# A state-space mixer with an MLP gate: the second group's rows in two transfers, and another order of the instructions

## The chip, the core and the metric

The kernel runs on one core of a Trainium2 chip. The core has five instruction streams that matter here: TensorE (PE: matmuls; its weight loads are shown apart, as PEld), VectorE (DVE), ScalarE (ACT), GpSimd (POOL) and SyncE (SP, which here only issues DMA transfers). Each stream runs its instructions in the order in which they were written, and waits on semaphores for the others. The metric is the time of one execution on the device in microseconds (us); a kernel's time is the median of its runs.

## What is computed

For 2048 tokens of width D = 448 the kernel normalises x, runs the result through a diagonal complex recurrence (A) and, separately, through a second normalisation and an MLP with F = 1792 (B), and gates one with the other. Cut to what matters:

```python
def _A_ref(x, ...):                       # the recurrence over the tokens
    dt = jnp.exp(log_dt)
    Lam_bar = jnp.exp(dt * Lam)
    B_bar = ((Lam_bar - 1.0) / Lam)[:, None] * Bmat
    Bu = einsum("bld,pd->blp", x, B_bar)
    h_t = Lam_bar * h_{t-1} + Bu_t
    return 2.0 * einsum("bld,dp->bld", h, Cmat).real + x * Dskip

def _B_ref(x, w1, b1, w2, b2):
    h = gelu(layernorm(x) @ w1 + b1)
    return h @ w2 + b2

xn = layernorm(x)
out = x + _A_ref(xn, ...) * silu(_B_ref(xn, ...))
```

## The kernel before

**Tiling.** The 2048 tokens are 8 blocks of 256; two blocks are a group, and there are four groups. In a block the even and the odd tokens ("par" 0 and 1) form the two halves of 128 rows, one token pair in each partition. Each group goes through the same stages:

- *Rows in.* `ldx` (a DMA that SP issues; every plain transfer is recorded by the helper at L84) brings x to `x_all`. Block 0 comes as two transfers, block 1 as one, and from then on two blocks come in one transfer of 448 KB.
- *Normalisation.* Statistics (L401, aggregated at L407; L431 and L432 for the first group), the scale (L478 to L488; Ln and Exp on ACT at L434, L435, L438 and L439 for the first group), and its application to `xn_sb` and `xn2_sb` (L499 on VectorE or L500 on ACT; L453 for the first group). The normalised rows are transposed to `xnT` and `xn2T`, for the first group's MLP by TensorE (L460, copied out at L419), otherwise by DMA (helper L83).
- *MLP.* `mm1_run` (L809) multiplies by w1 in phases: 64-row matmuls, six of the first kind and eight of the second, into a pair of PSUM banks. The gelu (L813, two activations on ACT) empties the pair, and only then can the next phase start on it. There are three such pairs. `mm2` (L836) has 14 matmuls for each 128 rows, into bank 5 or 6; then VectorE adds b2 (L839) and the silu follows (on ACT, or as tanh on ACT and a product on VectorE).
- *Recurrence.* `bu` (L737, bank 4) gives Bu, copied out by L419. `ssm` (L752 to L783) is a long chain on VectorE: products, the scans (L761, L763), copies to `s_b` (L419 on ACT or VectorE), and products again into `h_sb` (L779, L781, L783).
- *Output.* `ym` multiplies h by C (L879 for par 0, with L882; L879 with L885 for par 1) into bank 7 (in the last group 7, 4 and 0). VectorE takes it from there (L891, L893, L896), an add (L899) brings x in, and SP sends the rows out. The products xn times Dskip (`xd`, L855 and L856) and, for the last one, L864 serve the odd rows.

Once, between the first and the second group's work, the kernel makes the tables of the recurrence, the matrices `BT`, `CQ` and `CZ`, and the matrix M0 (L720 for the first three quarters; `m0_halves`, L705, for the last one, whose operand is CQ and whose bank 7 is emptied by VectorE and ACT).

**What sets the order.** Nothing is emitted where it is written. Each piece of work becomes a task of a `Plan`: an engine, one or more instructions, and the names of what it reads and writes. `link` derives the dependencies from these names. `emit` (L127 to L159) then goes through the list `ORDER` (L162 to L184), 634 task numbers, and puts each task's instructions on its engine with the semaphore waits that its dependencies need. A task recorded with `either` has a second engine to run on; `SECOND` (L185 to L188) lists the 60 tasks that take it. So these two lists alone decide what each engine does, and in which order:

```python
for t in order:
    eng, seen = self.engs[t.eng], self.seen[t.eng]
    ...
    for sem, val in reversed(waits):
        eng.wait_ge(self.sems[sem], val)
    ...
    for k, fn in enumerate(t.ins):
        last = fn(eng)
```

**The start.** TensorE runs warm-up matmuls (L422, on `ones`; 26, 12, 5 and 5 of them) around the first small jobs: the transposes of the parameters Lambda_re, Lambda_im and log_dt (L529, L530), the transposes of the first normalised rows (L460) and b1's columns (L602, L603). ACT issues the three parameter transfers, loads the table for Ln and Exp (L316), and later that for gelu (L443).

**The loads on SP.** x of blocks 0 and 1, then w1 in eight transfers, then `ldx(2, 2, S1 + 7)` (L377, blocks 2 and 3), then w2 in four, then B and C.

Of the kernel before, what the change touches and what calls it, by code (L numbers as in the profile page):

```python
# [155 lines left out]
def dram_ap(t, offset, ap):  # L156
    return bass.AP(tensor=t.tensor, offset=offset, ap=ap)
# [2 lines left out]


ORDER = [int(k) for k in """  # L162
# [17 lines left out]
""".split()]  # L180
SECOND = [int(k) for k in """
46 54 55 62 64 67 70 75 77 84 108 113 131 134 159 161 163 164 166 178 185 186 188 190 191 221 223 225 227 229 231 239 249 250 259 267 269 332 363 365
366 385 401 402 437 448 469 481 483 488 492 500 502 503 505 511 529 530 610 613
""".split()]  # L184


# [14 lines left out]
def bass_recurrent_scan__ssm_conv_s5__mixer_channel_mlp__prompt_kernel(  # L201
# [18 lines left out]
    with ExitStack() as es:  # L220
# [85 lines left out]
        with nc.Block():  # L306
# [26 lines left out]
            def ld(eng, o, i, writes, nbytes, prio, reads=(), dur=0.45):  # L333
                kb.dma(eng, o, i, reads=reads, writes=writes, prio=prio, nbytes=nbytes, dur=dur)
# [4 lines left out]
            def ldx(b0, n, prio, reads=(), eng="sp"):  # L339
                ld(eng, x_all[:, b0:b0 + n, :, :], dram_ap(A_x, b0 * 256 * D, [[2 * D, 128], [256 * D, n], [D, 2], [1, D]]),  # L340
                   [f"x{b}" for b in range(b0, b0 + n)], n * 256 * D * 2, prio, reads, dur=0.25 + 0.2 * n)
# [16 lines left out]
            S1 = 10 * PINNED  # L358
# [12 lines left out]
            for c, (a, n) in enumerate(CH):  # L371
# [2 lines left out]
            ld(("pool", "sp")[0], dbc[:], dram_ap(A_Dskip, 0, [[0, 128], [1, D]]), ["dbc"], 114688, -20, reads=[] if 0 else ["sgn3", "w1r_3"])  # L374
            kb.either(("act", lambda e: e.activation(dbc[:], dbc[:], ACT.Copy, scale=0.5), 0.6, 0.2),
                      ("dve", lambda e: e.tensor_scalar(dbc[:], dbc[:], 0.5, None, op0=ALU.mult), 0.2, 0.12), ["dbc"], ["dbc"], -20)
            ldx(2, 2, S1 + 7)  # L377
            CK = []

            def ldc():  # L380
# [592 lines left out]
            for step in STEPS.split():  # L973
                k, g, a = step[0], int(step[1]), step[2:]
# [54 lines left out]
```

## Time and profile before

| | |
|---|---|
| median of 3 runs | 153.82 us (153.58 to 154.24) |
| the profiled execution | 153.63 us |
| its span | 151.9 us, and 1.73 us around it |
| TensorE granted clock | 1.00 |
| the span's chain on TensorE, by line | L809 29.1%, L836 28.2%, L737 14.3%, L879 12.3%, L882 4.0% |
| bytes moved by DMA | 14.73 MB, 97 GB/s in the mean |

Busy time of an engine is the time in which it runs instructions; issuing DMA transfers is not counted. The chain of waits is followed back from the last instruction: at each step to what released it, or to the instruction ahead of it on its engine. Where the chain stays on one engine, that engine's own work sets the time, and other engines matter only where they make it wait. A row of a timeline has the start, the duration, the engine, the line, the operation, output and inputs with their shapes, the number of instructions, and in brackets the idle time before it with what ended it.

### The profile page before, as it was taken

How to read it: one execution, taken by the hardware profiler on the slowest of the kernel's cores; microseconds unless marked ns; L12 is line 12 of the kernel's file. 1: busy time of each engine (PE TensorE's matmuls, PEld its weight loads, DVE VectorE, ACT ScalarE, POOL GpSimd, SP SyncE). 2: the span in 40 equal slices, each digit the busy share in tenths (PEclk: the TensorE clock that was granted, in tenths of full speed). 3: DMA queues.
4: the chain of work that ended last, by engine and by line, in shares of the span. 5: the costliest groups of instructions: out<-in, count | busy, mean ns of one | idle time of the engine just before them, and what ended most of it. 6: DMA issues, size and time to landing. Idle time of an engine off the chain costs nothing.

```text
span 151.9 us, 2990 instructions
## 1 busy us (share of the span) xinstructions
PE 147.6 (97%) x1136; PEld 87.5 (58%) x1136; DVE 128.2 (84%) x270; ACT 98.4 (65%) x182; POOL 40.8 (27%) x100
## 2 busy tenths in 40 slices
PE   7999999999999999999999999999999999999992
PEld 7886755444566577545444556754444666555561
DVE  3978969899998969999999996379968727999984
ACT  3787998888789559997798610462579833067400
POOL 5377870053021910010366006200071040000200
PEclk9999999999999999999999999999999999999999
DMA  4999999889996100700003032610340001100022
GB/s 117 270 309 389 262 231 182 175 150 154 214 213 165 23 0 0 138 0 4 0 0 63 4 60 53 146 60 4 60 109 14 4 0 60 60 0 0 4 102 79
DMA packets 31236, 14.73 MB, mean 97 GB/s; under 512 B 24752, under 2 KB 30774, under 8 KB 31222
## 3 DMA queue, kind: packets, MB, share of 16 engines
q1 hardware_dynamic: 30912, 14.26, 41.9%
q0 software_dynamic: 160, 0.23, 0.6%
q8 instruction: 9, 0.15, 0.4%
q10 hardware_dynamic: 150, 0.05, 0.1%
q14 instruction: 5, 0.04, 0.1%
HBM read 6.89 MB, written 1.84 MB: 57 GB/s over the span
## 4 chain that ended last, share of the span: by engine, by line
PE 96%; DVE 2%; issue 0%; DVEq 0%
PE psum L809 29%; PE psum L836 28%; PE psum L737 14%; PE psum L879 12%; PE psum L882 4%; PE psum L422 3%; PE psum L720 3%; PE psum L885 1%; DVE t L893 1%; PE psum L460 1%; DVE tmp L899 1%; PE psum L705 1%; PE psum L602 0%; DVE ones L309 0%; PE psum L529 0%
## 5 line engine op out<-in xcount | busy, mean ns | idle before, releaser
L809 PE MATMUL psum<-xn2T,w_sb 64*128 64x512 bf16 (+1 forms) x462 | 44.6, 345 | 0.2
L836 PE MATMUL psum<-w_sb,gT 128*128 128x448 bf16 x224 | 44.4, 353 | 0.0
L813 ACT ACTIVATE gT<-psum,b1f 128x512 bf16<-128x512 f32 (+1 forms) x66 | 36.0, 625 | 10.6 <-PE psum L809 10.4
L809 PEld LDWEIGHTS psum<-xn2T,w_sb 64*128 64x128 bf16 x462 | 24.0, 109 | 19.7 <-ACT gT L813 2.3
L836 PEld LDWEIGHTS psum<-w_sb,gT 128*128 128x128 bf16 x224 | 21.6, 98 | 20.3 <-issue 0.6
L419 ACT ACTIVATE u_sb<-psum 128x512 bf16<-128x512 f32 (+2 forms) x22 | 10.5, 478 | 23.0 <-PE psum L737 22.7
L737 PE MATMUL psum<-xnT,BT 128*128 128x256 bf16 x196 | 24.0, 273 | 0.0
L737 PEld LDWEIGHTS psum<-xnT,BT 128*128 128x128 bf16 x196 | 18.9, 98 | 5.4 <-issue 1.1
L761 DVE TENSOR_TENSOR_SCAN s_w<-dk,vs 128x774 f32<-128x774 f32 x8 | 14.0, 1760 | 0.1
L899 POOL TENSOR_TENSOR tmp<-t,x_all 128x448 bf16<-128x448 bf16 x5 | 5.2, 1031 | 33.1 <-DVE t L896 30.7
L500 ACT ACTIVATE xn_sb<-x_all,lnw 128x448 bf16<-128x448 bf16 (+2 forms) x21 | 13.0, 661 | 1.2 <-DVE xn_sb L499 1.1
L419 ACT ACTIVATE vs<-s_w 64x256 bf16<-64x256 f32 (+2 forms) x16 | 10.9, 682 | 2.6 <-DVE s_w L761 1.5
L879 PE MATMUL psum<-CZ,h_sb 128*128 128x448 bf16 x56 | 11.9, 353 | 0.0
L839 DVE TENSOR_TENSOR o<-psum,b2bc 128x448 f32<-128x448 f32 x16 | 9.7, 614 | 1.7 <-PE psum L836 1.5
L879 PE MATMUL psum<-CQ,h_sb 128*128 128x448 bf16 (+2 forms) x54 | 10.5, 332 | 0.0
L879 PEld LDWEIGHTS psum<-CZ,h_sb 128*128 128x128 bf16 x56 | 5.4, 98 | 4.7 <-DVE lnmv L407 0.4
L401 DVE BATCH_NORM_STATS2 lnst<-x_all 128x6 f32<-128x448 bf16 x12 | 7.0, 614 | 0.6 <-DMA x_all<-in_A_x_dram 0.6
L879 PEld LDWEIGHTS psum<-CQ,h_sb 128*128 128x128 bf16 x54 | 5.1, 98 | 4.0 <-DVE t L893 0.4
L882 PE MATMUL psum<-M,xnT 128*128 128x448 bf16 x32 | 7.4, 352 | 0.0
L891 DVE TENSOR_TENSOR Cr<-psum,xd 128x448 f32<-128x448 f32 x7 | 4.3, 620 | 3.5 <-PE psum L885 3.4
L480 POOL TENSOR_TENSOR lnw<-lnw,mhalf 128x8 f32<-128x8 f32 x3 | 7.0, 2332 | 0.3
L499 DVE TENSOR_SCALAR xn_sb<-x_all,lnw 128x448 bf16<-128x448 bf16 (+2 forms) x19 | 6.9, 395 | 0.0
(160 smaller groups left out, 189.8 us busy)
## 6 DMA issues: line engine op xcount, KB each, us to landing
out_dram<-tmp SPq DMA_DIRECT2D x7, 224.0 KB, 2.0
x_all<-in_A_x_dram SPq DMA_DIRECT2D x3, 448.0 KB, 4.3
w_sb<-in_B_w_dram SPq DMA_DIRECT2D x3, 448.0 KB, 8.5
w_sb<-in_B_w_dram SPq DMA_DIRECT2D x3, 384.0 KB, 4.9
vs<-in_A_C_re_dram SPq DMA_DIRECT2D x1, 392.0 KB, 11.5
Bn<-in_A_B_im_dram SPq DMA_DIRECT2D x1, 336.0 KB, 10.4
Bn<-in_A_B_re_dram SPq DMA_DIRECT2D x1, 336.0 KB, 10.8
vs<-in_A_C_im_dram SPq DMA_DIRECT2D x1, 336.0 KB, 11.3
```

What stands on the lines that cost most here:

```text
L401: dve([lambda e, b=b, par=par, q=q: e.bn_stats(lnst[:, q, :], x_all[:, 2 * g + b, par, :])], [f"x{2 * g + b}"] , [f"st{q}"], 0.62, prio)
L419: kb.either(("act", [lambda e, o=o, i=i: e.activation(o, i, ACT.Copy) for o, i in pairs]), ("dve", [lambda e, o=o, i=i: e.tensor_copy(o, i ...
L480: power = fns + [lambda e: e.tensor_tensor(w(2), w(0), mhalf[:].to_broadcast([128, 2, nq]), ALU.pow), lambda e: e.tensor_tensor(w(3), mean ...
L500: ("act", [lambda e, o=o, i=i: e.activation(o, i, ACT.Identity, bias=nb, scale=rs) for o, i in parts], 0.75, 0.2)]
L737: fns = [lambda e, r=r, m=m, d=d: e.matmul(psum[:, 4, r * NK:(r + 1) * NK], BT[:, m, d, :], xnT[:, gx, d, :], start=(d == 0), stop=(d == 6 ...
L761: dve(lambda e, so=so, vi=vi: e.tensor_tensor_scan(so, dk[:].rearrange("p i c -> p (i c)"), vi, 0.0, ALU.mult, ALU.add), ["v", "vl", "dk", ...
L809: return lambda e: e.matmul(view(bk[k]), w1_sb[rows, d, fcol(2 * j + k)], rhs[rows, d, :, :], start=not second and n == 0, stop=second and ...
L813: act([lambda e, k=k: e.activation(gT[:, gb, 2 * j + k, :].rearrange("p (r c) -> p r c", r=2)[:, :, cols], view(bk[k]), ACT.Gelu_apprx_tan ...
L836: fns = [lambda e, fi=fi: e.matmul(psum[:, bk, 0:D], gT[:, gb, fi, q * 128:(q + 1) * 128], w2_sb[:, fi, :], start=(fi == 0), stop=(fi == N ...
L839: dve(lambda e: e.tensor_tensor(o2[:, fb, :], psum[:, bk, 0:D], b2bc[:], ALU.add), [f"ps{bk}", "b2bc"], [f"oo{fb}"], 0.62, prio - 76)
L879: fns = [lambda e, k=k: e.matmul(psum[:, bk, c0:c1], h_sb[:, hb, k, k0:k0 + 128], cm[:, k, c0:c1], start=(k == 0), stop=False) for k in ra ...
L882: fns += [lambda e, d=d: e.matmul(psum[:, bk, c0:c1], xnT[:, gx, d, xs], M0[:, d, c0:c1], start=False, stop=(d == 3)) for d in range(4)]
```

## The change

The one load of blocks 2 and 3 becomes two loads of one block each, so that block 2's work can start when its own half is there. One task more is recorded (635), so the numbers of the tasks behind it grow by one, and the lines behind L377 too (L809 becomes L810). The lists `ORDER` and `SECOND` are new throughout; `SECOND` has 71 entries now.

```diff
 ORDER = [int(k) for k in """
-1 14 20 0 48 10 17 19 21 15 2 95 27 18 96 92 28 93 22 16 25 49 5 97 13 109 94 91 110 98 105 104 26 106 100 23 99 50 51 56 6 52 66 107 3 111 101 112 57
...
+13 0 49 10 16 92 20 96 6 26 97 3 14 19 17 25 93 15 1 21 94 5 27 101 18 23 2 50 95 98 106 110 51 107 111 99 52 102 113 105 53 100 108 112 109 28 54 55
...
 SECOND = [int(k) for k in """
-46 54 55 62 64 67 70 75 77 84 108 113 131 134 159 161 163 164 166 178 185 186 188 190 191 221 223 225 227 229 231 239 249 250 259 267 269 332 363 365
...
+46 53 55 65 68 69 73 76 78 79 82 84 85 86 87 88 90 91 112 132 135 158 160 163 165 179 186 189 191 192 222 224 226 228 230 232 236 238 240 242 248 260
...
-            ldx(2, 2, S1 + 7)
+            for a in (2, 3):
+                ldx(a, 1, S1 + 7)
```

What the new lists do, found by setting the two orders side by side:

- **TensorE** has the same 1136 instructions. At the start the 26 and 12 warm-up matmuls come in one go, then the parameters' transposes, both transposes of block 0, b1's columns, and the last ten warm-up matmuls. The first six L836 matmuls stand ahead of the last six phases (36 matmuls) of the first group's L809. L705 stands before one L836 (14 matmuls) and seven L737 that it followed. The last L836 of the third group stands before the last group's L809, and the L737 of that group's odd-sized tile comes earlier; the outputs of the last two groups are in a slightly different order.
- **ACT** loads its first table before it issues the transfer of log_dt. It has 176 instructions instead of 186.
- **VectorE** has 285 instructions instead of 270. It takes 18 tasks from ACT (five of the scalings at L666, five L500, copies of u and `s_b` and some others) and 21 from POOL (two adds L899, two products L855 and L856, and column-sized operations), and gives 12 tasks to ACT and 16 to POOL (four L856, one L899, the add at L864, and small ones).
- **POOL** has 91 instead of 96, **SP** 60 instead of 59.

More of the change, by code (lines that the diff above doesn't have):

```diff
@@ L162 @@
 ORDER = [int(k) for k in """
[17 rows of a table removed]
[17 rows of a table added]
 """.split()]
 SECOND = [int(k) for k in """
-46 54 55 62 64 67 70 75 77 84 108 113 131 134 159 161 163 164 166 178 185 186 188 190 191 221 223 225 227 229 231 239 249 250 259 267 269 332 363 365
-366 385 401 402 437 448 469 481 483 488 492 500 502 503 505 511 529 530 610 613
+46 53 55 65 68 69 73 76 78 79 82 84 85 86 87 88 90 91 112 132 135 158 160 163 165 179 186 189 191 192 222 224 226 228 230 232 236 238 240 242 248 260
+261 262 268 271 352 354 381 405 446 448 449 452 470 471 481 484 485 489 501 506 507 509 514 527 528 532 533 574 611
 """.split()]
```

32 rows, old and new, of the table ORDER are left out of this document.

## The prediction

> **What bounds the kernel now.** I read the busy times first, then the chain of waits, then stretches of the span.
>
> ```profile
> span 151.9 us, 2990 instructions
> PE 147.6 (97%) x1136; PEld 87.5 (58%) x1136; DVE 128.2 (84%) x270; ACT 98.4 (65%) x182; POOL 40.8 (27%) x100
> ...
> PE 96%; DVE 2%; issue 0%; DVEq 0%
> ```
>
> TensorE is busy for 97% of the span and is the chain for 96% of it; VectorE, at 84%, is the only engine near it. So time can be won only where TensorE waits, and lost wherever an order makes it wait more. The windows by stage (columns: window, length, then busy time of PE, PEld, DVE, ACT, POOL, granted clock, DMA share, GB/s) say where it waits:
>
> ```profile
> 0.00:7.17 7.17, 6.00 (x68) 5.62 (x69) 4.28 (x14) 3.60 (x11) 3.33 (x17) 1.00 0.68 187
> 7.17:19.30 12.13, 12.00 (x176) 8.91 (x176) 10.31 (x41) 10.81 (x24) 8.96 (x26) 1.00 1.06 317
> 19.30:67.50 48.20, 48.20 (x338) 27.77 (x336) 43.64 (x98) 40.06 (x72) 11.84 (x33) 1.00 0.72 128
> ...
> 147.50:151.90 4.40, 1.35 (x15) 1.01 (x12) 2.21 (x6) 0.00 (x0) 0.00 (x0) 1.00 0.31 104
> ```
>
> Before 7.17 us TensorE runs warm-up matmuls while the inputs are normalised; after 147.5 VectorE finishes the last outputs. Between them PE has no gap, at a granted clock of 1.00. Busy is not full cadence, though. The undisturbed pace is readable from the chain: 56 L836 matmuls in 10.70 us are 0.191 each; 14 L737 in 1.53 are 0.109 each. Against such paces, matmul groups after 7.17 lose only about 3.2 us in all: roughly 0.1 at each change between 64-row (L809) and 128-row matmuls, and the rest in a few short waits, most of them at the end of the first group's L809:
>
> ```profile
> 7.17 2.48 PE psum L809 x42
> 9.65 0.55 PE psum L460 x8
> 10.20 7.49 PE psum L809 x102
> 17.69 0.05 issue
> 17.74 0.97 PE psum L809 x14
> 18.71 0.05 issue
> 18.76 0.63 PE psum L809 x8
> 19.39 10.70 PE psum L836 x56
> ```
>
> The two "issue" steps are where the first group's gelu (L813 on ACT) has not freed a PSUM pair: in the weight-load rows the idle gaps before 17.73 and 18.76 are 0.32 and 0.33. By the 0.054 us per matmul of an undisturbed eight-matmul phase (0.43), three phases there (17.17, 18.20, 18.76) lose 0.25, 0.23 and 0.13: 0.61 us. This is what an order can win at once.
>
> **The change, part by part.** PE keeps its 1136 instructions and every shape, so its 147.6 us of work is a floor that stays.
>
> *The split load.* Blocks 2 and 3 come in two transfers of 224 KB instead of one of 448 KB.
>
> ```profile
> 6.78 0.59 SPq L84 DMA_DIRECT2D x_all<-in_A_x_dram  x1
> 12.15 2.21 DVE L401 BATCH_NORM_STATS2 lnst<-x_all 128x6 f32<-128x448 bf16 x4 [0.44 <-DMA x_all<-in_A_x_dram]
> ```
>
> The old transfer is issued at 6.78 and lands at 12.13, where VectorE has waited 0.44 for it. At the 317 GB/s of that stretch half of it is 0.7 us, so block 2 should land near 11.5 and the 0.44 goes. What it feeds is not on the path: these statistics lead to the normalised rows whose transposes PE needs at 30.0 and which landed at 27.24, 2.8 us early. One more issue costs SP 0.59, and every SP transfer behind it (w2, B, C) is issued that much later; but SP runs ahead of the data here (w2's four pieces are issued by 9.30 and land 14.16 to 18.51, needed from 19.3), and the bytes are the same. So 0; without that cover, 0.6 at most, or 0.44 gained at best.
>
> *The start.* ACT now loads its table (1.28) before it issues log_dt; this DMA moves from 1.37 to about 3.0. PE runs 26+12 warm-up matmuls in one go, then the parameter transposes, both x transposes without five matmuls between them, and ten warm-up ones. ACT makes the first half's scale (two activations, 0.53) before the second's, and VectorE puts one block-1 statistic (0.62) ahead of the two normalisations:
>
> ```profile
> 4.44 0.40 DVE L453 TENSOR_SCALAR xn_sb<-x_all,lnmv,lnw 128x448 bf16<-128x448 bf16 x1
> 4.75 0.62 DVE L431 BATCH_NORM_STATS2 lnst<-x_all 128x6 f32<-128x448 bf16 x1
> 5.29 0.38 DVE L453 TENSOR_SCALAR xn_sb<-x_all,lnmv,lnw 128x448 bf16<-128x448 bf16 x1
> ...
> 6.60 0.42 DVE L419 COPY xn2T<-psum 128x512 bf16<-128x512 bf16 x1 [0.17 <-PE psum L460]
> ```
>
> Statistics end at 4.52; first scale 5.08, second 5.57, second normalisation to 5.95 instead of 5.67. The transposes follow at once, to 6.55. VectorE has a statistic and an aggregate in between, so its copy ends near 7.25 instead of 7.02, and L809 starts near 7.40: **+0.23**. The gelu table load ends 0.4 later (9.0); the pair that this gelu frees is next wanted at 10.8, against about 10.7 ready: 0.
>
> *The first L836 in pieces.* Six of the first 14 L836 matmuls (6 x 0.19 = 1.13 us) move ahead of the last six L809 phases, 36 matmuls. That is work PE does while ACT catches up, so the 0.61 goes: ACT still has L500 rows (2.06 for three) among these gelus. It costs two more shape changes at 0.1: **-0.61 + 0.20**. Their w2 piece landed at 15.34; PE comes there near 16.9, so it is there even after one more SP issue.
>
> *Work moved between engines.* By the rows of each kind, VectorE takes 18 tasks from ACT (16.2 us there) and 21 from POOL (9.9), and gives 12 (6.6 on VectorE) to ACT and 16 (4.1) to POOL. What it takes runs faster there (an L499 0.40 against 0.66 for L500; an L899 0.42 against 1.03), so VectorE grows by about 3.5 us to 131.7, ACT falls to about 91. Neither reaches 147, so the totals cost nothing; slack at single points counts. I followed each of VectorE's values up to the PE step that needs it, with the old durations in the new queue. Most have 0.5 us or more left. Tight ones: L705 (M0's last quarter) stands ahead of one L836 and seven L737 now, 3.4 us earlier, and its operand is ready with 0.05 left (0.7 before); L783's second half for the second group's first output has 0.3 (0.7 before); that of the last group 0.06 (0.26 before). I charge **+0.08** for these. The last outputs keep their order on VectorE:
>
> ```profile
> 147.65 0.51 DVE t L893
> ...
> 149.47 0.42 DVE tmp L899
> ```
>
> so the tail stays. A mishap could be one late by a whole VectorE instruction: 0.4 to 0.7 at each.
>
> One pattern speaks against the change: where POOL's and VectorE's two-input operations run together, both stretch.
>
> ```profile
> 111.45 1.44 DVE L896 TENSOR_TENSOR t<-Cr,g_sb 128x448 bf16<-128x448 f32 x1 [1.15 <-POOL tmp L899]
> 113.35 1.20 DVE L763 TENSOR_TENSOR_SCAN s_w<-cw,cur,vs 128x256 f32<-128x256 f32 x1
> ```
>
> The same L896 takes 0.62 at 109.69, the same scan 0.74 elsewhere: +0.82 and +0.46. Now four L856 products go to POOL, one beside the chain before L783. *By the Trainium skill ("SBUF — State Buffer", "Who interferes with whom") a VectorE instruction with two SBUF inputs and GpSimd exclude each other for a whole instruction; the trace agrees as far as these rows go, and by that rule each such meeting costs VectorE up to POOL's 1.03.* POOL's total falls by about 2 us, so there are not more meetings in sum, and I charge nothing; the rival below does.
>
> **Sum.** +0.23 - 0.61 + 0.20 + 0.08 = -0.10 us. The profiled execution took 153.63, its span 151.9 with 1.73 around it; it stands 0.19 below the median of 153.82. So span 151.8, and **153.7** as the median.
>
> **The rivals.** Chances in brackets, 0.42 for the forecast (its own range 153.2 to 154.4).
>
> *B, faster (0.22).* The start is no later, since PE's free run of transposes and VectorE's earlier copies absorb the 0.23, and other first-stage waits go with the 0.61: 0.13 at 10.14 and 0.14 at 34.57. -0.10 - 0.23 - 0.27, and one of the two shape changes free (-0.10), is -0.7: **153.1**, to 152.8 if an add of the tail that POOL takes over (L864, about 0.3 on VectorE) is time won. For it: PE's waits sit just there. Against it: the copy rests on a queue I could follow instruction by instruction.
>
> *C, slower (0.26).* VectorE, with 3.5 us more, comes late at L705, at L783 of the second and of the last group, because locks like those above (0.46 to 0.82) exceed slacks of 0.05, 0.3 and 0.06. All three by 0.64 in the mean: 0.59 + 0.34 + 0.58 = 1.5; the first and the last alone give 1.17, in place of the 0.08 charged: 153.7 + 1.1 = **154.8**; all three and a POOL add beside L893 in the tail (0.4) give 153.7 - 0.08 + 1.5 + 0.4 = 155.5. It decides once these waits exceed 0.9 together. Against it: most late values are caught up, as PE takes other work first.
>
> *D, log_dt late (0.10).* Issued at 3.0 after the table load, and with the 2.0 us minimum from issue to landing in this trace, it lands at 5.0 or later, while PE, after its 38 warm-up matmuls, stands before the parameter transposes from about 5.3; both x transposes (wanted at 5.7) are behind them. A landing at the x transfers' median 2.4 after an issue at 3.2 gives 5.6 plus: 0.1 to 0.8 late, **154.2** at 0.5.
>
> *That the split does nothing* gives the forecast's number, since it was priced at 0.
>
> **How the numbers follow.** A change of under 0.5% (0.77 us) can hardly be told from none here. Faster: B and 0.02 of the forecast, 0.24. Slower: C, half of D and 0.04 of the forecast, 0.35. Same: 0.41. The range reaches from B's end, 152.8, to C's end, 155.5.
>
> **What would show it.** L809's first row at 7.3 to 7.5; no issue step in the chain between 10 and 20 us and L836 appearing near 17; the L401 rows from 11.6 without the DMA wait; DVE near 132, ACT near 91; L705 near 60.4 with no gap in PE. PE's weight loads waiting for DVE at L705 or L879 would mean C; PE idle before L530 means D. I am wrong if PE's busy share drops below 96.5%, or if the time moves by more than 0.77 us from another stage than the first 20 us.

## The result, and the profile after

| | before | after |
|---|---|---|
| median | 153.82 us (153.25 to 154.47, 7 runs) | 155.63 us (154.44 to 156.49, 7 runs) |
| profiled execution | 153.63 us, span 151.9 | 154.78 us, span 152.6 |
| spans of all runs, median | 152.0 (151.5 to 152.9, 29 runs) | 153.4 (152.3 to 154.3, 7 runs) |
| time around the span, median | 1.74 us (29 runs) | 2.18 us (7 runs) |

The change made the kernel slower: ratio 1.0104, 95% interval 1.0065 to 1.0144. The loss of 1.81 us in the medians is 1.4 us of span and 0.4 us around it. The profiled execution of the changed kernel is one of its shorter ones, with 0.7 us of span lost: what the profile shows is about half of the span lost in the median. The changed kernel has seven runs from one session; the 29 of the kernel before were made beside the first experiments.

The lines that answer to those shown of before come first, from the page of the changed kernel:

```profile
span 152.6 us, 3000 instructions
PE 147.5 (97%) x1136; PEld 87.3 (57%) x1136; DVE 132.2 (87%) x285; ACT 91.7 (60%) x172; POOL 40.0 (26%) x95
...
PE 66%; DVE 24%; DMA 4%; issue 2%; ACT 1%; SPq 0%; DVEq 0%; ACTq 0%
```

PE has the same work, but the chain of waits that was 96% PE is now 66% PE, 24% VectorE and 4% DMA: something other than PE set the end for a while. The windows by stage (columns as before) say where:

```profile
7.37:20.34 12.97, 12.97 (x185) 9.60 (x184) 11.92 (x43) 11.50 (x26) 8.05 (x24) 1.00 1.07 319
20.34:48.00 27.66, 27.66 (x204) 15.24 (x204) 23.39 (x59) 23.82 (x39) 8.88 (x27) 1.00 0.98 173
48.00:68.00 20.00, 19.39 (x129) 11.85 (x127) 19.35 (x40) 14.14 (x30) 5.70 (x8) 1.00 0.26 50
68.00:108.78 40.78, 40.78 (x277) 22.20 (x277) 36.59 (x68) 20.03 (x36) 8.79 (x14) 1.00 0.24 42
```

PE is idle for 0.61 us between 48 and 68, and nowhere else between its first L810 and its last matmul:

```profile
48.88 0.36 PE L721 MATMUL psum<-CQ,Bn 128*128 128x448 bf16 x1 [0.61 <-DVE CQ L670]
```

The chain of waits up to there, read from its DMA step on:

```profile
38.95 0.44 SPq L83
39.39 0.04 issue
39.44 4.08 DMA x_all<-in_A_x_dram
...
43.54 1.68 DVE lnst L402 x3
...
45.65 0.58 DVE CQ L670
...
47.57 0.60 DVE CQ L670
48.17 0.09 DVE lnmv L408
48.26 0.58 DVE CQ L670
48.84 0.05 issue
48.88 1.50 PE psum L721 x7
```

The transfer of blocks 4 and 5 (not the one that was split) leaves SP at 39.44, behind the same four transposes of BT as before; before it left at 37.92. Of these 1.5 us, 0.62 are a small piece of B (64 rows) that now precedes the four, and 0.89 are the four themselves (6.40 against 5.51 us); why they took longer is not shown. The transfer lands at 43.52. On VectorE three statistics of these blocks stand ahead of the last three CQ products, and its timeline shows that it stood there:

```profile
41.15 0.68 DVE L670 SCALAR_TENSOR_TENSOR CQ<-Cr,cw,tmp 128x448 bf16<-128x448 bf16 x1
43.54 1.68 DVE L402 BATCH_NORM_STATS2 lnst<-x_all 128x6 f32<-128x448 bf16 x3 [1.72 <-DMA x_all<-in_A_x_dram]
```

The order of before had a statistic ahead of the last three CQ products too, but there the transfer landed 0.20 after VectorE came for it:

```profile
42.26 0.63 DVE L401 BATCH_NORM_STATS2 lnst<-x_all 128x6 f32<-128x448 bf16 x1 [0.20 <-DMA x_all<-in_A_x_dram]
```

The statistics serve the third group, whose first L810 starts at 68; but the products CQ2, CQ4 and CQ6 stand behind them in the same queue, and the first L721 (M0) needs all seven CQ. PE's milestones in the two profiled executions (L809 and its successors, starts in us):

| | first L809 | end of first group's L809 | second group's first L809 | first M0 | third group's first L809 | end of the last matmul |
|---|---|---|---|---|---|---|
| before | 7.17 | 19.39 | 30.02 | 48.40 | 67.51 | 148.85 |
| after | 7.37 | 20.34 | 29.84 | 48.88 | 68.00 | 149.34 |

At 30 us the change is 0.18 ahead; at the first M0 it is 0.48 behind, and it stays 0.49 behind to the last matmul. The other 0.2 us come behind the last matmul. The last output transfer is issued 1.08 us after it in both (149.93 and 150.42), but SP then waits longer for the outputs to land, first before, then after:

```profile
SPq L153 <- DMA out_dram<-tmp: 1.2, 1, 1.2
SPq L153 <- DMA out_dram<-tmp: 1.5, 1, 1.5
```

It is so in every trace: 1.2 or 1.3 us in the five of the order of before and its variants, 1.4 to 1.7 in the ten of the new order. The output ahead of the last three leaves later now (148.03, before 146.81), so more of the bytes are under way at the end; that this is the cause was not tested.

### The profile page after: what moved, and what is told of

Its sections match the earlier page's. It is cut to its first block, busy times and chain, and to the rows that moved or that the text cites. A ratio compares the mean times of both kernels' runs of the same rounds, so it can differ in the third digit from the quotient of the medians.

```text
span 152.6 us, 3000 instructions
## 1 busy us (share of the span) xinstructions
PE 147.5 (97%) x1136; PEld 87.3 (57%) x1136; DVE 132.2 (87%) x285; ACT 91.7 (60%) x172; POOL 40.0 (26%) x95
## 4 chain that ended last, share of the span: by engine, by line
PE 66%; DVE 24%; DMA 4%; issue 2%; ACT 1%; SPq 0%; DVEq 0%; ACTq 0%
PE psum L810 21%; PE psum L837 19%; PE psum L738 10%; PE psum L880 7%; DMA x_all<-in_A_x_dram 4%; PE psum L721 3%; PE psum L883 2%; DVE tmp L668 2%; DVE s_w L762 2%; DVE CQ L670 2%; DVE o L840 2%; DVE tmp L900 2%; DVE lnst L402 1%; DVE Bn L670 1%; DVE t L897 1%
## 5 line engine op out<-in xcount | busy, mean ns | idle before, releaser
L810 PE MATMUL psum<-xn2T,w_sb 64*128 64x512 bf16 (+1 forms) x462 | 44.2, 345 | 0.0
L810 PEld LDWEIGHTS psum<-xn2T,w_sb 64*128 64x128 bf16 x462 | 24.1, 109 | 19.2 <-issue 2.1
L501 ACT ACTIVATE xn_sb<-x_all,lnw 128x448 bf16<-128x448 bf16 (+2 forms) x20 | 12.5, 659 | 0.7 <-DVE xn_sb L500 0.4
L842 ACT ACTIVATE g_sb<-o 128x448 bf16<-128x448 f32 x8 | 4.6, 570 | 9.2 <-DVE o L840 9.1
L420 ACT ACTIVATE vs<-s_w 64x256 bf16<-64x256 f32 (+2 forms) x9 | 6.9, 771 | 3.8 <-DVE s_w L762 3.6
L845 DVE SCALAR_TENSOR_TENSOR g_sb<-th,o 128x448 bf16<-128x448 f32 x8 | 4.9, 614 | 2.0 <-ACT th L844 2.0
L500 DVE TENSOR_SCALAR xn_sb<-x_all,lnw 128x448 bf16<-128x448 bf16 (+2 forms) x20 | 6.6, 365 | 0.0
```

Of the source, the lines that this page charges most:

```text
L420: kb.either(("act", [lambda e, o=o, i=i: e.activation(o, i, ACT.Copy) for o, i in pairs]), ("dve", [lambda e, o=o, i=i: e.tensor_copy(o, i ...
L501: ("act", [lambda e, o=o, i=i: e.activation(o, i, ACT.Identity, bias=nb, scale=rs) for o, i in parts], 0.75, 0.2)]
L810: return lambda e: e.matmul(view(bk[k]), w1_sb[rows, d, fcol(2 * j + k)], rhs[rows, d, :, :], start=not second and n == 0, stop=second and ...
```

## The experiments

All are orders of the same tasks. The runs whose names begin with b_ start from the order of before, those with a_ from the changed one. The pattern of the diffs: rows of one engine's queue, with "-" where a task stood and "+" where it went. "CI" is the 95% interval of the ratio to the kernel before. A pair such as (0,1) is a pair of PSUM banks, CQ5 or BT1 a piece of that matrix; lines behind L377 are one higher where the load is split.

| run | ratio (CI) | median us | span, median | around, median |
|---|---|---|---|---|
| b_split | 0.9988 (0.9969 to 1.0007) | 153.50 | 151.8 | 1.73 |
| a_onedma | 1.0071 (1.0048 to 1.0094) | 154.91 | 152.8 | 2.14 |
| a_stats_late | 1.0005 (0.9989 to 1.0020) | 154.03 | 152.1 | 1.97 |
| a_x4_early | 1.0045 (1.0026 to 1.0063) | 154.63 | 152.4 | 2.17 |
| b_early836 | 1.0042 (1.0026 to 1.0059) | 154.45 | 152.7 | 1.76 |
| a_no836 | 1.0045 (1.0019 to 1.0071) | 154.23 | 152.4 | 1.89 |
| a_start | 1.0005 (0.9983 to 1.0026) | 153.93 | 152.1 | 1.86 |
| b_x4_late | 1.0251 (1.0197 to 1.0304) | 158.19 | 156.4 | 1.79 |
| a_best | 1.0030 (1.0012 to 1.0048) | 154.23 | 152.3 | 1.92 |
| b_best | 0.9971 (0.9955 to 0.9987) | 153.27 | 151.6 | 1.74 |
| a_dbc_late | 1.0045 (1.0022 to 1.0069) | 154.76 | 152.6 | 2.14 |
| a_two_late | 1.0012 (0.9988 to 1.0036) | 154.04 | 152.1 | 1.91 |
| a_all | 1.0024 (1.0003 to 1.0044) | 154.27 | 152.4 | 1.88 |

**Split or order?** b_split is the order of before with the two loads; a_onedma is the new order with the one load.

```diff
 b_split, SP
-x of blocks 2 and 3, 448 KB
+x of block 2, 224 KB
+x of block 3, 224 KB
```

> The order of before with the split load alone: blocks 2 and 3 in two transfers, the second right behind the first on SP, everything else as before. Theory (the loss sits in the order, not in the split): block 2 lands near 11.5 instead of 12.13, VectorE's 0.44 wait for it goes, PE unchanged; ratio to before 0.997 to 1.003. Rival (the split itself costs, as one more transfer ahead of w2, B and C on SP, or as one more transfer to close at the end): 1.005 to 1.010, with PE waiting for w2 or a later stage, or with more than 1.73 us of time around the span.

> The new order with the old single transfer for blocks 2 and 3. Theory (the loss sits in the order): as slow as the change, 1.007 to 1.013, with PE's wait for CQ ahead of the first L721 (0.6 us in the changed kernel) still there. Rival (the split costs): back to 1.000 or below. The time around the span, 2.18 us in the changed kernel against 1.73 before, tells which of the two it belongs to.

The split alone is not distinguishable from no change. Its one profile does show the rival's sign, PE waiting for w2, whose last piece landed at 19.65 (18.51 before):

```profile
PE psum L837 <- DMA w_sb<-in_B_w_dram: 0.7, 1, 0.7
```

But in b_best (below), with the same two loads, that piece landed at 17.57 and PE did not wait, and the median of b_split's spans is no longer than that of before; so this wait is not there in every execution, and the split is not shown to cause it. The order alone costs 0.5 to 0.9%, with PE's wait for CQ (0.7 us in its profile) in it; PE also waited 0.6 there for the first normalised rows. So most of the loss belongs to the order. Whether the split adds something in the new order is open: the intervals of a_onedma and of the change overlap, and their medians are 0.7 us apart. The time around the span (2.14) goes with the order too.

**The wait behind the statistics.** Two ways to take it away, from two sides of it.

```diff
 a_stats_late, VectorE
 L670 CQ5
-L402 and L408, blocks 4 and 5 (eight tasks, between the CQ)
 L670 CQ2 ... CQ4 ... CQ6
+L402 and L408, blocks 4 and 5
```

> The changed kernel with the four statistics and four aggregates of block 4 and 5 (L402, L408) moved behind the last CQ (L670) on VectorE; nothing else moves. Theory (VectorE stood 1.7 us before the transfer of blocks 4 and 5 with CQ queued behind it, and PE then waited 0.6 for CQ): PE's wait goes, every later PE instruction is 0.7 earlier, span near 151.9, ratio to before 1.003 to 1.006. Rival (CQ is late anyway, by VectorE's added work): VectorE's wait only moves, PE still waits 0.4 or more, ratio unchanged at 1.010.

```diff
 a_x4_early, SP
 L83 BT0, BT3
+x of blocks 4 and 5
 L83 BT1, BT4
-x of blocks 4 and 5
 L83 BT2, BT5
```

> The changed kernel with the transfer of blocks 4 and 5 two transposes earlier on SP (issued near 36.8 instead of 39.4), VectorE's queue as it is. Theory: it lands near 40.9, before VectorE asks for it at 41.8; VectorE's 1.7 us wait and PE's 0.6 go, ratio 1.003 to 1.006. Rival (two transposes of BT are now late and PE waits for them instead): a gap before L738 at 42.4 of 0.3 or more, ratio 1.008 or more.

With the statistics late, the span is 152.1 in the median and 1.3 of the 1.4 us is back. That is more than the theory gave (1.003 to 1.006) and twice the 0.6 to 0.7 us that the wait cost in the profile, so a part of it has another source, which is not shown. The spans also vary less (151.6 to 152.4 over twelve runs, against 152.3 to 154.3); but a_no836 and a_start, which have the late statistics too, reach 154.0 and 153.2, so the narrow spread is not owed to them alone. In its profile CQ6 ends at 46.63 and the first M0 follows its neighbour at 48.25 without a gap:

```profile
45.36 1.27 DVE L670 SCALAR_TENSOR_TENSOR CQ<-Cr,cw,tmp 128x448 bf16<-128x448 bf16 x2
46.55 1.67 DVE L402 BATCH_NORM_STATS2 lnst<-x_all 128x6 f32<-128x448 bf16 x3
```

The earlier transfer takes the wait for CQ away as well, and the ratio lies in the theory's range; but the rival's wait came with it: BT is now late, and PE waits 0.4 us for it (from the table of PE's waits of that run):

```profile
PE psum L738 <- DMA BT<-Bn: 0.4, 1, 0.4
```

So moving the transfer pays on one side and costs on the other, and moving the statistics costs nothing that a run shows. The reverse, the suspected cost alone in the kernel before:

```diff
 b_x4_late, SP
 L83 BT, four
-x of blocks 4 and 5
 L83 BT, three
+x of blocks 4 and 5
```

> The order of before with the transfer of blocks 4 and 5 behind three more transposes on SP (issued near 42.4 instead of 37.9, landing near 46.4); VectorE's queue is untouched. This is the suspected cost alone and larger. Theory: VectorE, which asks for it at 42.1, waits 4.1 us more with CQ3's successors queued behind; the last CQ ends near 50.8 instead of 47.28 (a wait of 0.54 before it goes), PE stands 2.3 us before the first L720, ratio 1.012 to 1.018. Rival (VectorE catches up, as PE is the bound): PE's wait under 1 us, ratio under 1.007.

```profile
46.34 0.63 DVE L401 BATCH_NORM_STATS2 lnst<-x_all 128x6 f32<-128x448 bf16 x1 [4.06 <-DMA x_all<-in_A_x_dram]
```

VectorE waited 4.06 and PE 2.0 (2.3 had been expected), and this execution had a span of 154.3. Its other three runs had spans of 156.4 to 156.5, which no trace shows; the ratio of 1.025 is larger than either theory gave.

**A second wait of the same kind.** The change also put the scaling of Dskip (L376) early on VectorE, where it waits for its own transfer (0.52 us in the changed kernel's profile, 1.0 in one experiment and 1.9 to 2.0 in two, as that transfer landed between 19.8 and 22.1).

```diff
 a_dbc_late, VectorE (a_two_late: this and a_stats_late)
 L637 three
-L376 dbc
 L640, L655, L500, L840, L562, L565, L574
+L376 dbc
```

> The changed kernel with one task moved: VectorE's scaling of Dskip (L376), which the change put where VectorE reaches it at 19.9 us and waits for its transfer (landings of 19.8 to 22.1 in the traces so far), goes seven instructions later, behind the first add of b2. The statistics stay where the change has them. Theory (this second wait delays VectorE, and with it CQ, by an amount that varies from run to run): the wait at 20 us goes, VectorE reaches the statistics sooner but still stands before them until the transfer of blocks 4 and 5 lands; CQ still late, ratio 1.004 to 1.009, between the change (1.0104) and the run with late statistics (1.0005). Rival (it costs nothing, as the wait for blocks 4 and 5 absorbs it): ratio 1.010 as before.

> Both moves: late statistics and late Dskip. Theory (both waits of VectorE on transfers cost): ratio 0.997 to 1.000, span no longer than 152.0, no wait of PE for VectorE. Rival (with the statistics late, VectorE has catching up enough): 1.0005 as in the run with late statistics.

a_dbc_late lies between the change and a_stats_late, though its interval touches the change's; PE still waited 0.8 for CQ. With the statistics late, moving L376 too brings nothing (1.0012 against 1.0005). So moving the statistics is enough to bring the lost span back, and L376 can at most feed the same delay.

The profile of a_dbc_late is the one trace of a longer execution of an order so near to the change (span 153.7, 1.1 more than the changed kernel's). There the inputs land later: PE waits 0.3 for the first normalised rows and 0.3 for a piece of w1, its first L810 starts at 7.68, the second group's at 30.59 (29.84 in the changed kernel) and the first M0, behind a wait of 0.83 for CQ, at 49.85 (48.88). So of the 1.1 us about 0.75 arise in the first 30 us, 0.6 of them as these two waits, and 0.2 in a longer wait for CQ.

**The early L836.** The forecast put 0.61 us on PE's waits at the end of the first group's L809, and expected the six early L836 to fill them.

```diff
 b_early836, PE (a_no836 is the reverse, in a_stats_late)
 L809 phases
+L836 x6
 L809 x6 pair (0,1), L809 x8 pair (0,1), L809 x6 pair (4,7), L809 x8 pair (4,7)
-L836 x6
 L836 x50
```

> The order of before with one task moved on PE: the first six L836 matmuls go ahead of the first L809 phase that waits for gelu (17.2 us). Theory (that piece of the change is a gain, as forecast): the three waits of 0.25, 0.23 and 0.13 go, two shape changes of 0.1 come, the second group's first L809 starts 0.4 earlier than at 30.02, and as later stages are PE-bound it lasts: ratio 0.996 to 0.999. Rival (the gelus only finish when they do, and PE waits later, ahead of the remaining L836): start of the second group unchanged, ratio 1.000.

> The changed kernel with late statistics (the fourth run above) and the first six L836 matmuls back behind all of the first group's L809. Theory: PE loses 0.4 in the first 30 us against that run, so ratio to before 1.002 to 1.005 (that run: 1.0005). Rival (the piece brings nothing in this order, whose ACT queue differs): same start of the second group, ratio 1.0005.

(The "fourth run" of that text is a_stats_late.) b_early836 was slower, and its weight-load rows show why the forecast's reading was wrong. The waits are still there, unchanged, though PE comes 1.1 us later and ACT has finished the gelus ahead of them at 17.56:

```profile
18.82 0.15 PEld L809 LDWEIGHTS psum<-xn2T,w_sb 64*128 64x128 bf16 x4 [0.33 <-PE psum L809]
19.84 0.15 PEld L809 LDWEIGHTS psum<-xn2T,w_sb 64*128 64x128 bf16 x4 [0.33 <-PE psum L809]
...
27.89 0.11 PEld L836 LDWEIGHTS psum<-w_sb,gT 128*128 128x128 bf16 x2 [0.95 <-DVE o L839]
```

The releaser is PE itself: the second phase of a pair waits on a semaphore for the end of its first phase, and in the order of before the two stand next to each other, which costs about 0.23 each time. The change's order puts the two first phases ahead of the two second ones; that removed these waits, not the L836: in a_no836, without the early L836, PE's own waits are gone as well. What the L836 cover in the changed order is an ACT wait of 0.3 that a_no836 then shows (0.5 lost at that phase). The third line is the price in the order of before: VectorE's first add of b2 comes 1.1 us later, the work queued behind it is shifted, and the second add holds up an L836 for 0.5.

**The start.**

```diff
 a_start (in a_stats_late), ACT and VectorE; a_best: the second part too
-scale of half 0, scale of half 1; statistic of block 1, two applications
+scale of half 1, scale of half 0; application, statistic of block 1, application
 a_best, PE
-both transposes, b1's columns, ten warm-up matmuls, L810
+transpose, five warm-up, transpose, five warm-up, b1's columns, L810
```

> The changed kernel with late statistics, and the normalisation of block 0 back in the sequence of before: the scale of the half whose statistics come first is made first on ACT, its application, transposes and copy come first, and one statistic of block 1 moves between the two applications on VectorE; the warm-up matmuls stay where the change put them. Theory (the later start of L809 comes from this sequence): first L809 at 7.15 to 7.25 instead of 7.37, everything after that 0.15 to 0.2 earlier, ratio 0.998 to 1.000. Rival (the ten warm-up matmuls behind b1's columns now set the start): first L809 at 7.3 or later, ratio unchanged at 1.0005.

> The changed kernel with late statistics, the normalisation sequence of before (as in the run before it), and on PE five warm-up matmuls between the two transposes of block 0 and five right behind them, so that none stands between b1's columns and the first L809, which is one that does not write b1's bank. Theory (what made L809 start at 7.4 to 7.6 is the ten warm-up matmuls behind b1's columns): first L809 at 6.8 to 7.1, 0.4 to 0.6 earlier than the run with late statistics, of which half or more reaches the end; ratio 0.996 to 0.999. Rival (VectorE's copies set the first L809, or the gelu table, whose load ends near 9.0, stops PE at the first reuse of a pair): PE waits for gelu near 10.5, ratio 1.000.

Both theories missed: the first L810 stayed at 7.51 and 7.50. In a_start the transposes were done at 6.2, but b1's columns had to wait 0.4 for b1's transfer and the ten warm-up matmuls followed; in a_best that was gone, and w1's 64-row piece for the first phase, which the change had moved from second to third place on SP, landed at 7.37. a_best also waited 0.3 for a b2 add behind L376. The last run takes both away:

```diff
 a_all: a_best, with L376 late, and on SP
 w1, 3x512
+w1, 64x512
 w1, 64x256
-w1, 64x512
```

> Both moves, and the start of the tenth run with w1's 64-row piece for the first L809 phase issued second instead of third on SP, as before the change. Theory (in the tenth run that piece landed at 7.37 and set the start at 7.50, and L376's wait to 22.2 cost 0.3 before an L837): first L810 near 6.9, no wait before L837, span 151.3 to 151.7, ratio 0.995 to 0.999. Rival (another input sets the start): first L810 at 7.3 or later, ratio 0.999 to 1.003.

(The "tenth run" of that text is a_best.) The piece landed at 6.43 and the first L810 still began at 7.42: PE's own queue reached it only then, as the parameter transposes, which stand behind 38 warm-up matmuls, started at 5.28 (4.00 before). So at least three things hold the start of the new order near 7.4, and none alone is its cause. Single traces cannot separate such small steps: with the start of before unaltered, the first L809 came between 6.82 and 7.39 in five traces, and with the change's between 7.37 and 7.68 in seven.

**A version that beats both.** It takes from the change what the runs showed to be good, and keeps the order of before for the rest.

```diff
 b_best: b_split, and on PE
 L809 x6 pair (0,1)
+L836 x6
+L809 x6 pair (4,7)
 L809 x8 pair (0,1)
-L809 x6 pair (4,7)
 L809 x8 pair (4,7)
-L836 x6
 b_best, VectorE
-L840, L637, L565, L637, L640, four others, L840
+L637, L565, L637, L840, L640, L840, four others
```

> The order of before with the split load; the six early L836 matmuls and the last pair's first L809 phase stand between the two phases of one pair, which before follow each other directly; and on VectorE the first two adds of b2 (L839) move behind two and before one table operation, so that the second add is not queued 1.1 us behind the first. Theory (the waits of 0.25 and 0.23 are PE's wait for its own previous phase on the same pair, and the loss of the run with early L836 alone was VectorE's second add): both waits go, no wait for L839 comes, two shape changes of 0.1 stay; second group's first L809 near 29.7 from a start at 7.1, ratio 0.995 to 0.998. Rival (the add or the table operations behind it are late in any order): a wait before L836 or L809 of 0.3 or more, ratio 1.000 or more.

```profile
6.87:19.94 13.07, 13.07 (x183) 9.55 (x184) 10.19 (x40) 11.66 (x26) 9.72 (x30) 1.00 1.07 308
```

PE has no idle time in the first stage, the second group starts at 29.44, and the kernel is 0.13 to 0.45% faster than before: 153.27 us. From the first L810, at 6.87, that is 22.57 us, 0.28 less than before; the other 0.30 of the earlier second group is the earlier start, which varies between executions of this order. How much each of the three parts brings was not separated, and the interval overlaps that of b_split.

## Why the prediction was wrong

It gave 153.7 us (152.8 to 155.5) and "same" as likeliest; the median of 155.63 lies 0.13 above the range.

- **The step that failed is the price of the work moved between engines.** The forecast followed each VectorE value "with the old durations in the new queue", found that "most have 0.5 us or more left", and charged +0.08 for L705 and two L783. The CQ ahead of the first M0 is not among its tight points. That way of following a queue adds durations up; nowhere does the forecast ask when the x of blocks 4 and 5 lands, and of the transfers that SP issues later it names w2, B and C alone. The runs showed instead: this transfer left 1.5 us later, VectorE reached the statistic at 41.83, and it landed at 43.52. That is 1.72 us of VectorE and 0.61 of PE; a_stats_late takes the wait away and gives back 1.3 us of span in the medians.
- **Two terms were put at nothing that were not.** "So the tail stays" rests on VectorE's order alone; the wait for the last outputs grew from 1.2 to 1.5 us, 0.2 to 0.3 of the loss. And the 1.73 us around the span were carried over without a reason; 2.18 was measured, 0.4 of the loss. With 1.73 the median would be near 155.1 (153.4 + 1.73), inside the range, and the forecast's mechanism would be as wrong.
- **The first stage came out right in size, in part by luck.** The forecast had -0.18 at the second group's start (without the 0.08), and so it was measured. From the first L809 to there the time fell from 22.85 to 22.47, by 0.38 (forecast 0.41), but for another reason: the 0.61 was read as gelu not freeing a pair, and two of its three parts (0.25 and 0.23) were PE waiting for its own previous phase, as the releaser named in the row said. The start came 0.20 later (forecast 0.23), but not through VectorE's copy alone, and the kernel before has starts from 6.82 to 7.39: that the two single traces lie 0.20 apart is luck.
- **The split** cost nothing measurable in the order of before, as forecast: block 2 landed at 11.59 (forecast 11.5). In the new order its cost is open.
- **The engines' totals** came out as worked: VectorE 132.2 (131.7), ACT 91.7 (91). L706 started at 60.96 and PE had no idle time there or at the outputs; none of the three tight points of rival C held it up. C's direction was right, its place and mechanism were not.
- **The collisions** of VectorE and POOL moved, and did not grow. L897 on the same operands took 0.61 to 0.63 in all four rows (1.44 in one before), but L756 took 1.07 once (0.41 elsewhere), L753 1.55 once (0.96), and L894, beside POOL's L864 in the tail, 0.96 (0.62). VectorE's rows that took over 0.15 us longer than the median of their kind lost 1.9 us in all (2.2 before). That "both stretch" is not in the rows that the forecast shows: POOL's adds beside them took their usual 1.03; in the changed kernel two took 1.42 and 1.68. By the rule of the Trainium skill ("SBUF — State Buffer", "Who interferes with whom") the one that comes second waits for a whole instruction; the largest loss of VectorE beside an add of POOL, 0.65 at L756, is below that add's 1.68, so these rows do not speak against it, and PE waited for none of them.
- **Rival D** (log_dt late behind the table load) fell; the issue ran beside the load:

```profile
1.62 1.28 ACT L316 ACT_TABLE_LOAD   x1 [1.62 <-PEq L1015]
1.65 0.23 ACTq L84 DMA_DIRECT2D dk<-in_A_log_dt_dram  x1
```

- **What stays open:** the time around the span. It is 2.08 to 2.23 in the changed kernel and 1.69 to 1.90 in the kernel before, and between 1.8 and 2.3 in every variant of the new order; variants of the old order have 1.70 to 1.88. No row of a trace covers that time. Open, too, is what makes the changed kernel's longer executions longer, as its profile is of a shorter one; in a_dbc_late's it was late inputs more than the wait for CQ.

## What to carry to other kernels

When an order of instructions changes, ask for each instruction that reads a transfer when its engine reaches it and when the transfer lands, not only when it was issued: here a statistic of the third group, which PE starts at 68 us, stood at 42 us for 1.72 us before a late transfer, with all of VectorE's queue behind it. Look behind the last matmul as well, where no engine is busy. Read the releaser before pricing a wait: a wait for the engine's own previous work goes away by interleaving, not by filler. And an engine at 87% busy can still set the end through one instruction.

## What had not been expected of the hardware

A second phase of L809 on the PSUM pair of the phase directly ahead loses 0.23 to 0.25 us of PE, the same when it comes at 17.7 and at 18.8 us (weight-load gaps of 0.32 and 0.33). A DMA issue on ACT started 0.03 us after the start of a table load of 1.28. The landing of one 112 KB transfer issued by POOL varied from 6.4 to 8.1 us after its issue between variants of the same order (19.79 from 13.36, 22.14 from 14.03).
